# Decode attention on one core: a 0.5 MB weight block loads behind the last values, the TensorE program gets shorter and its opening is ordered by hand

## The chip, the cores and the metric

One NeuronCore of a Trainium2 chip runs the whole kernel. Its engines work side by side and each runs its own instructions in order: TensorE (PE: matrix products, with the weight loads shown as PEld), VectorE (DVE), ScalarE (ACT), GpSimd (POOL) and SyncE (SP), which here only issues transfers. Transfers run on sixteen DMA engines. Data comes from HBM into SBUF, matrix products land in PSUM. The metric is the device time of one execution in microseconds (us): the median of several runs. The profile is one further execution, with the time of every instruction.

## The reference

One token (`x`, 512 values) passes an attention layer over a window of 4096 cached positions for 32 heads of 128, and a small gating network.

```python
xn = layernorm(x)
q = (xn @ wq).reshape(32, 128)                  # wq: 512 x 4096
k, v = k_cache[:, -4096:, :], v_cache[:, -4096:, :]   # 32 heads x 4096 x 128, bf16
p = softmax(q . k * 128**-0.5)                  # per head, over 4096 positions
s = concat(p @ v) @ wo                          # wo: 4096 x 512
h = gelu(layernorm(xn) @ w1); hs = shift(h) @ w2
x1 = xn + hs                                    # with one token the shifted h is all zeros
g = silu(x1 + gelu(layernorm(x1) @ w3) @ w4)    # w3: 512 x 1376
out = x + s * g
```

The window is 32 MB of keys and 32 MB of values, each read once.

## The kernel before

The 32 heads are worked in eight groups of four (`G = 4`). A group's keys are one tile `kv` of 128 partitions by 128 columns of 128 values (4 MB); its values are another. A stage `s` of the main loop takes the keys of group `s` and the values of group `s - 2` (`LAG = 2`).

**Scores.** The first `nd(g)` columns of a group go to DVE in four parts: `k_vector` multiplies by the query (L321) and adds up (L323). The other columns go to PE and ACT in batches of at most eight: `k_turn` transposes on PE (L339) and copies on ACT (L342), `k_scores` multiplies (L350). `nd` is 64 for group 0 and for group 7, 80 for the rest. `sm_own` (ACT, L359), `sm_max` (DVE, L364 and L366), `sm_turn` (PE L372, DVE L374 and L376) and `sm_exp` (PE L381, ACT L384 and L388) make the exponentials `pT`. `sm_den` (PE, L394) adds their sums over partitions and `sm_rden` (DVE, L399) inverts them, once a group.

**Values.** `v_wide` (PE, L427) multiplies `pT` with the values into the one accumulator `ov`, ACT copies it (L433), `v_turn` transposes it (PE, L444), `v_add` adds (DVE, L450) and `v_out` scales by the inverted sum (L471 on DVE for the later groups). The last group is different: its values come in three pieces by the column bounds `cuts`; the last piece goes through `v_part` (PE, L461), straight into the output tile `oT`.

**Output weights.** `wo` is used in four blocks of heads: 0-15, 16-23, 24-27 and 28-31. For the first three, `ox_spread` (DVE, L482) and `ox_pick` (PE L490, DVE L492 and L496) rearrange the heads' outputs to fit the layout in which `wo` was loaded, and `y_wide` (PE, L518) multiplies into the row accumulator `yr`; ACT copies that into `y_sum` (L640), and `rows_add` (PE, L155) adds it to `y_ps`. The last four heads are multiplied singly by `y_head` (PE, L155). Then DVE multiplies by the gate (L651), adds `x` (L653), and the result is stored.

**Order.** All large loads but `wq` go through one helper on SP's queue (L76), in program order: `w2`, `w3`, `w4`, then keys and values as the stages ask for them, each held back until its buffer is free. Key tiles have three buffers, of which one is given to `wo` of heads 0-23 from stage 5 on; value tiles have two, in the space of the opening's weights (`wts`). `wq` goes through ACT's queue. In the main loop the order on PE, DVE and ACT is that of the program (`manual_schedule`). Ahead of the loop (layer norm, query, gate network) Tile's scheduler orders the instructions. Most short PSUM results share one buffer, `misc`: an instruction that writes into it waits until the one before has been read.

**Warm-up.** `warm(3)` (L507) issues three products with zeros, 128 x 512, once ahead of the values of group 6 and once ahead of those of group 7.

Of the kernel before, what the change touches and what calls it, by code (L numbers as in the profile page):

```python
# [8 lines left out]
P = 128  # L9
# [9 lines left out]
G = 4  # L19
# [7 lines left out]
def kernel(  # L27
# [153 lines left out]

    x_f = small.tile([P, KC], FP32, name="x_f")
# [16 lines left out]

    q_row = wts.tile([P, H // G, 2, Dh], BF16, name="q_row")  # L200
    q_bc = small.tile([P, H // G, Dh], BF16, name="q_bc")
    qr = [ps_tr.tile([P, 4, Dh], FP32, tag="pt", name="qr_ps") for _ in range(2)]
    for b in range(2):
        zeros(qr[b][:])
        for c in range(KC):
            wc = wq_sb[:, c, :].rearrange("p (g a d) -> p g a d", a=G, d=Dh)
            for a in range(G):
                nc.tensor.matmul(qr[b][32 * a:32 * a + 1], lhsT=xq_bf[:, c:c + 1], rhs=wc[:, 4 * b:4 * b + 4, a, :],  # L208
                                 start=False, stop=(c == KC - 1), skip_group_check=True)
    nc.scalar.copy(out=q_row[:, 0:4, 0, :], in_=qr[0][:])  # L210
    nc.vector.tensor_copy(out=q_row[:, 4:8, 0, :], in_=qr[1][:])  # L211
    for b in range(2):
        qb_ps = ps_tr.tile([P, 4, Dh], FP32, tag="pt", name="qb_ps")
        nc.tensor.matmul(qb_ps[:], lhsT=sel[:].rearrange("k b a -> k (b a)"), rhs=q_row[:, 4 * b:4 * b + 4, 0, :],
                         start=True, stop=True)
        nc.scalar.copy(out=q_bc[:, 4 * b:4 * b + 4, :], in_=qb_ps[:])
# [11 lines left out]
    shifted_bf = small.tile([P, KC], BF16, name="shifted_bf")  # L228
    nc.vector.memset(shifted_bf[:], 0.0)
    hs_ps = ps_misc.tile([P, KC], FP32, tag="misc", name="hs_ps")  # L230
    for j in range(KC):
        for c in range(KC):
            nc.tensor.matmul(hs_ps[:, j:j + 1], lhsT=w2_sb[:, c, j::4],
                             rhs=shifted_bf[:, c:c + 1], start=(c == 0), stop=(c == KC - 1))
    x1_f = small.tile([P, KC], FP32, name="x1_f")
    nc.vector.tensor_tensor(out=x1_f[:], in0=xn_f[:], in1=hs_ps[:], op=ALU.add)
    xc3, _, rstd3 = ln_stats(x1_f[:], "z3")
    z3_bf = small.tile([P, KC], BF16, name="z3_bf")
    nc.vector.tensor_scalar(out=z3_bf[:], in0=xc3[:], scalar1=rstd3[:], scalar2=None, op0=ALU.mult)

    xn_row = small.tile([P, P], FP32, name="xn_row")
    nc.vector.tensor_scalar(out=xn_row[:], in0=x_row[:], scalar1=negmean[:], scalar2=rstd[:],
                            op0=ALU.add, op1=ALU.mult)

    a_ps = ps_misc.tile([P, 3, P], FP32, tag="misc", name="a_ps")
    zeros(a_ps[:])
    for c in range(KC):
        wc = w3_sb[:, c, 0:10 * P].rearrange("p (q r) -> p r q", r=10)
        parts = [(j, a_ps[32 * j:32 * j + 1, :, :], wc[:, 3 * j:3 * j + 3, :]) for j in range(3)]
        parts += [(3, a_ps[96:97, 0, :], wc[:, 9, :]), (3, a_ps[96:97, 1, 0:96], w3_sb[:, c, 10 * P:F])]  # L250
        for j, dst, w in parts:
            nc.tensor.matmul(dst, lhsT=z3_bf[:, c:c + 1], rhs=w, start=False, stop=(c == KC - 1),
                             skip_group_check=True)
    a_row = wts.tile([P, 3, P], BF16, name="a_row")
    nc.scalar.activation(out=a_row[:], in_=a_ps[:], func=ACT.Gelu_apprx_tanh)  # L255
    at_ps = ps_misc.tile([P, 3, P], BF16, tag="misc", name="at_ps")
    for m in range(3):
        nc.tensor.transpose(at_ps[:, m, :], a_row[:, m, :], ident_bf[:])
    a_bf = small.tile([P, 3, 4], BF16, name="a_bf")
    nc.vector.tensor_copy(out=a_bf[:], in_=at_ps[:, :, 0:P:32])  # L260

    hr_ps = ps_misc.tile([P, KC, P], FP32, tag="misc", name="hr_ps")
    zeros(hr_ps[:])
    terms = [(shifted_bf[:, c:c + 1], w2_sb[:, c, :]) for c in range(KC)]
    for i in range(11):
        n = P if i < 10 else 96
        terms.append((a_bf[0:n, i % 3, i // 3:i // 3 + 1], w4_sb[0:n, i, :]))
    for i, (col, w) in enumerate(terms):
        r = 32 * (i % 4)
        nc.tensor.matmul(hr_ps[r:r + 1].rearrange("r j n -> r (j n)"), lhsT=col, rhs=w, start=False,  # L270
                         stop=(i >= len(terms) - 4), skip_group_check=True)
# [10 lines left out]

    make_masks(16)
    make_masks(8)
    make_masks(4)

    y_ps = ps_y.tile([P, P], FP32, name="y_ps")
    rows_open(y_ps)  # L290

# [16 lines left out]
    def nd(g):  # L308
        return 64 if g == 0 or g >= LATE else 80
# [68 lines left out]
    def sm_exp(g):  # L378
# [7 lines left out]
        s["sum"] = sm_pool.tile([P, G], FP32, tag="sum", name="sum")  # L386
# [4 lines left out]
    def sm_den(g):  # L391
        s = st[g]
        s["den"] = ps_misc.tile([P, G], FP32, tag="misc", name="den_ps")
        nc.tensor.matmul(s["den"][:], lhsT=ones_f[:], rhs=s["sum"][:], start=True, stop=True)  # L394

    def sm_rden(g):
        s = st[g]
        s["rden"] = sm_pool.tile([P, G], FP32, tag="rden", name="rden")
        nc.vector.reciprocal(out=s["rden"][:], in_=s["den"][:])  # L399
# [64 lines left out]
    def v_out(g):  # L464
# [5 lines left out]
        if g >= NG - 5:  # L470
            nc.vector.tensor_tensor(out=o_blk[b][:, c:c + G], in0=st[g]["oT"][:], in1=st[g]["rden"][:],  # L471
                                    op=ALU.mult)
            return
# [30 lines left out]
    def warm(n):  # L504
        wm = ps_s.tile([P, 4, P], FP32, tag="sT", name="wm")
        for _ in range(n):
            nc.tensor.matmul(wm[:], lhsT=zero_bf[:], rhs=zero_bf[:].unsqueeze(1).to_broadcast([P, 4, P]),  # L507
                             start=True, stop=True)

# [12 lines left out]
    def y_head(h):  # L522
# [3 lines left out]
    cuts = (0, 64, 96, CP)  # L526
    region = tc.manual_schedule(engines={mybir.EngineType.PE, mybir.EngineType.DVE,
                                         mybir.EngineType.Activation})
    region.__enter__()
    v_pool = None  # L530
    for s in range(NG + LAG):
# [8 lines left out]
        if last:  # L540
            v = load_kv(v_pool, A_v_cache, h, cuts)
            for r in (H - G, H - 2):
                load_rows(r, 2)
        elif h >= 0:
            v = load_kv(v_pool, A_v_cache, h)
# [4 lines left out]
        if h == 5:  # L550
            load_wo(1)
            load_wo(2)

        if s < NG:
# [11 lines left out]
            if s == 7:  # L566
                v_turn(h - 1)
                v_add(h - 1)
                v_out(h - 1)
            elif s > 1:  # L570
                sm_den(s - 2)
                sm_rden(s - 2)
# [4 lines left out]
            if s == 7:  # L577
                sm_den(h)
                sm_rden(h)
# [38 lines left out]
        elif s == NG:  # L618
# [3 lines left out]
            y_wide(1, False)  # L622
            sm_den(NG - 2)
            sm_rden(NG - 2)
            y_wide(0, False)
            warm(3)
            v_wide(h, v)
            sm_den(NG - 1)
            sm_rden(NG - 1)
# [4 lines left out]
        else:  # L634
            v_open(h)
            warm(3)
            v_wide(h, v, cuts[1], last=False)
            ox_pick(2)
            y_wide(2, True)
            nc.scalar.copy(out=y_sum[:], in_=yr[0][:].rearrange("p j n -> p (j n)"))  # L640
            v_wide(h, v, cuts[2], cuts[1])
            v_turn(h)
            v_add(h)
            rows_add(y_ps, ind, y_sum, False)
            v_part(h, v, cuts[2], CP)
            v_out(h)
            for r in range(H - G, H):
                y_head(r)
    region.__exit__(None, None, None)
    y = small.tile([P, P], FP32, name="y")  # L650
# [34 lines left out]
```

## Time and profile before

| what | value |
|---|---|
| median of 3 runs | 193.45 us (193.33 to 193.55) |
| profiled execution, span from first to last instruction | 191.2 us |
| busy: PE, DVE, ACT | 116.4, 150.9, 89.2 us |
| moved by DMA | 79.02 MB, mean 413 GB/s over the span |
| mean granted TensorE clock | 0.72 |
| last piece of the last values in use on PE | from 186.38 us |
| `y_head` products | 187.59 to 188.01 us |
| store of the result issued | 188.68 us |

The profiled execution has a span of 191.2 us; the median lies 2.25 us above it, time outside the first and last instruction. Times in the views count from the span's start. A row of a timeline gives start, duration, engine, source line and operation, the tiles written and read, and in brackets how long the engine sat idle before it and what ended the wait. "PEclk" is the share of the full TensorE clock that was granted.

### The profile page before, as it was taken

To read this page: it belongs to the slowest core of one execution; us is meant where nothing else is said; L and a number is where in the kernel's file an instruction comes from. 1 tells how busy PE (TensorE), PEld (TensorE's weight loads), DVE (VectorE), ACT (ScalarE), POOL (GpSimd) and SP (SyncE) were. 2 spreads that over 40 slices of the span, in tenths; PEclk is the share of its full clock that TensorE was granted. 3 is DMA by queue.
4 is the path that set the end of the run, shared out by engine and by line. 5 is a ranking of instruction groups with operands and counts; after the bars stand their busy time and mean duration, and the time that the engine had idled before them with its cause. 6 is when DMAs were issued, how large, how long until landed. Compare 5 with 4: busy or idle time off the path is not lost.

```text
span 191.2 us, 2839 instructions
## 1 busy us (share of the span) xinstructions
PE 116.4 (61%) x1159; PEld 74.2 (39%) x1159; DVE 150.9 (79%) x175; ACT 89.2 (47%) x191; POOL 2.3 (1%) x11
## 2 busy tenths in 40 slices
PE   1653754989825368256845772680888189739762
PEld 0430222767614334143334441540763077313322
DVE  1660159979999999999999999999999999980111
ACT  2001370888794076427464564542475148733120
POOL 2110000000000000000000000000000000000000
PEclk9999695555755557955695588557567858975998
DMA  6999999999999999999999999999999998999990
GB/s 211 447 430 404 431 418 439 439 439 437 432 434 439 432 429 432 432 439 432 422 432 432 418 422 418 452 439 435 439 432 434 435 432 372 471 425 405 420 371 32
DMA packets 4572, 79.02 MB, mean 413 GB/s; under 512 B 624, under 2 KB 1232, under 8 KB 1488
## 3 DMA queue, kind: packets, MB, share of 16 engines
q1 hardware_dynamic: 4264, 74.65, 91.6%
q10 hardware_dynamic: 296, 4.20, 5.1%
q8 instruction: 9, 0.15, 0.3%
q14 instruction: 3, 0.02, 0.0%
HBM read 78.84 MB, written 0.00 MB: 412 GB/s over the span
## 4 chain that ended last, share of the span: by engine, by line
DVE 46%; DMA 43%; PE 5%; ACT 3%; issue 1%; SPq 1%; ACTq 0%; DVEq 0%
DMA kv<-in_A_k_cache_dram 31%; DVE S L323 28%; DVE prod L321 15%; DMA kv<-in_A_v_cache_dram 10%; ACT kt L342 3%; DMA x_bf<-in_A_x_dram 2%; PE pt L339 2%; PE ov L427 1%; DVE m L366 1%; DVE S L364 1%; SPq L76 1%; PE sT L350 1%; DVE mx L374 1%; PE oT L461 1%; PE ot_ps L444 0%
## 5 line engine op out<-in xcount | busy, mean ns | idle before, releaser
L323 DVE TENSOR_REDUCE S<-prod 128x20 f32<-128x2560 bf16 (+1 forms) x32 | 86.0, 2686 | 1.1
L342 ACT COPY kt<-pt 128x1024 bf16<-128x1024 bf16 x52 | 51.2, 1013 | 40.4 <-PE pt L339 38.7
L339 PE MATMUL pt<-ident_f,kv 128*128 128x128 f32 x208 | 46.7, 376 | 10.8 <-DMA kv<-in_A_k_cache_dram 10.8
L321 DVE TENSOR_TENSOR prod<-kv,q_bc 128x2560 bf16<-128x2560 bf16 (+1 forms) x32 | 45.4, 1418 | 3.9 <-DMA kv<-in_A_k_cache_dram 3.7
L339 PEld LDWEIGHTS pt<-ident_f,kv 128*128 128x128 f32 x208 | 34.2, 196 | 14.4 <-DMA kv<-in_A_k_cache_dram 10.5
L350 PE MATMUL sT<-q_pair,kt 128*128 128x8 bf16 x416 | 19.4, 170 | 15.7 <-ACT kt L342 15.5
L350 PEld LDWEIGHTS <-kt 128*128 128x128 bf16 x416 | 16.4, 104 | 26.8 <-ACT kt L342 25.8
L427 PE MATMUL ov<-kv,pT 128*16 128x512 bf16 x248 | 22.0, 515 | 1.4 <-DMA kv<-in_A_v_cache_dram 1.4
L388 ACT ACTIVATE pT<-S,mb 128x128 bf16<-128x128 f32 x32 | 13.9, 573 | 0.3
L372 PE MATMUL mt_ps<-ident_f,m 128*1 128x128 f32 x8 | 2.9, 359 | 17.4 <-DVE rden L399 16.9
L433 ACT COPY ov_sb<-ov 128x512 f32<-128x512 f32 x8 | 4.7, 586 | 17.1 <-PE ov L427 17.1
L427 PEld LDWEIGHTS <-pT 128*16 128x16 bf16 x248 | 6.9, 109 | 13.2 <-issue 11.4
L359 ACT ACTIVATE own<-sT,par 128x48 f32<-128x48 f32 (+1 forms) x32 | 7.5, 356 | 3.7 <-PE sT L350 3.7
L444 PE MATMUL ot_ps<-ident_f,ov_sb 128*128 128x128 f32 x32 | 7.1, 359 | 2.9 <-ACT mb L384 1.9
L211 DVE CAST q_row<-qr_ps 128x512 bf16<-128x512 f32 x1 | 0.7, 692 | 9.9 <-PE qr_ps L208 9.9
L388 ACT ACTIVATION_READ_ACCUMULATOR pT<-S,mb 128x1 f32 x32 | 8.3, 258 | 0.0
L372 PEld LDWEIGHTS mt_ps<-ident_f,m 128*1 128x1 f32 x8 | 0.6, 80 | 17.9 <-DVE rden L399 17.2
L399 DVE RECIPROCAL rden<-den_ps 128x4 f32<-128x4 f32 x8 | 1.4, 175 | 7.0 <-PE den_ps L394 7.0
L381 PE MATMUL mb_ps<-md,par_t 5*128 5x4 f32 x16 | 3.9, 311 | 4.1 <-DVE md L376 4.1
L255 ACT ACTIVATE a_row<-a_ps 128x384 bf16<-128x384 f32 x1 | 0.5, 491 | 12.0 <-remote 12.0
L444 PEld LDWEIGHTS ot_ps<-ident_f,ov_sb 128*128 128x128 f32 x32 | 4.5, 178 | 3.9 <-ACT mb L384 2.3
L208 PE MATMUL qr_ps<-wq_sb,xq_bf 128*1 128x512 bf16 x32 | 3.1, 566 | 3.7 <-DMA wq_sb<-in_A_wq_dram 3.7
(122 smaller groups left out, 81.6 us busy)
## 6 DMA issues: line engine op xcount, KB each, us to landing
kv<-in_A_k_cache_dram SPq DMA_DIRECT2D x7, 4096.0 KB, 31.3
kv<-in_A_v_cache_dram SPq DMA_DIRECT2D x7, 4096.0 KB, 30.6
wq_sb<-in_A_wq_dram ACTq DMA_DIRECT2D x1, 4096.0 KB, 17.6
kv<-in_A_k_cache_dram SPq DMA_DIRECT2D x2, 2048.0 KB, 27.4
wo<-in_A_wo_dram SPq DMA_DIRECT2D x1, 2048.0 KB
kv<-in_A_v_cache_dram SPq DMA_DIRECT2D x1, 2048.0 KB
kv<-in_A_v_cache_dram SPq DMA_DIRECT2D x2, 1024.0 KB, 17.6
w_sb<-in_B_w_dram SPq DMA_DIRECT2D x1, 1376.0 KB, 9.1
```

Source lines behind the costliest of these rows:

```text
L321: nc.vector.tensor_tensor(out=prod[:, 0:m, :], in0=kn[:, rows, :], in1=q_bc[:, g:g + 1, :].to_broadcast([P, m, Dh]), op=ALU.mult)
L323: nc.vector.tensor_reduce(out=st[g]["S"][:, rows], in_=prod[:, 0:m, :], axis=AX.X, op=ALU.add)
L339: nc.tensor.transpose(pt[:, i, :], kn[:, c:c + 2, :].rearrange("p c d -> p (c d)").bitcast(FP32), ident_f[:])
L342: nc.scalar.copy(out=kts[b][:, 0:n, :], in_=pt[:, 0:n, :].bitcast(BF16))
L350: nc.tensor.matmul(st[g]["sT"][:, c:c + 2, :].rearrange("p c a -> p (c a)"), lhsT=kt[:, i, l::2], rhs=q_pair[:, g, l, :], start=(l == 0), ...
L359: nc.scalar.mul(s["own"][:, 0:m, a], s["sT"][:, 0:m, a], par[:, a:a + 1])
L372: nc.tensor.transpose(mt_ps[:], s["m1"][:], ident_f[:])
L381: nc.tensor.matmul(mb_ps[:], lhsT=par_t[:].rearrange("k b a -> k (b a)"), rhs=md[:], start=True, stop=True)
L388: nc.scalar.activation(out=s["pT"][:, :, a], in_=s["S"][:], func=ACT.Exp, scale=scale, bias=mb[:, a:a + 1], accum_out=s["sum"][:, a:a + 1])
L427: nc.tensor.matmul(ov[r:r + 4 * G], lhsT=s["pT"][:, c:c + 4, :].rearrange("p i a -> p (i a)"), rhs=v[:, c:c + 4, :], start=(i < 4), stop=( ...
L433: nc.scalar.copy(out=s["ov_sb"][:], in_=ov[:])
L444: nc.tensor.transpose(ot_ps[:, step * j:step * j + P], s["ov_sb"][:, j, :], ident_f[:])
```

## The change

It has these parts.

1. **Load and products of `wo` of heads 24-27.** The 0.5 MB load is no longer issued in the stage of the values of group 5, but behind the three pieces of the last values and ahead of the two loads of `wo` for heads 28-31. Its products go singly into `y_ps`, between the last `v_out` and the `y_head` products, and no longer through `y_wide`. The `y_wide` of heads 16-23 moves from stage 8 to stage 9 and is the last into `yr`.
2. **Pieces of the last values**: bounds 64 and 104 in place of 64 and 96.
3. **No `warm`.**
4. **Group 0 gives 80 columns to DVE**, not 64.
5. **Denominators by pairs of groups**: `sm_den` runs for groups 1, 3, 5 and 7, makes the inverse for two groups, and `sm_rden` is gone. For groups 4 and 5 it stands in stage 7 between `v_add` and `v_out` of group 4.
6. **Opening.** PE and ACT follow program order from the layer norm on. The `w2` products are four rows of 512 with a copy and four transposes, and stay in the accumulator that the `w4` products then add to (before: sixteen products of width 1, and again four rows later). The `w3` products are sixteen, not twenty, with a different split of the 1376 columns; their transposes are two 32-bit ones. The program has the query's products behind the `w3` products.

```diff
+    order = tc.manual_schedule(engines={mybir.EngineType.PE, mybir.EngineType.Activation})
+    order.__enter__()
     x_f = small.tile([P, KC], FP32, name="x_f")
...
+    hr_ps = ps_s.tile([P, KC, P], FP32, tag="sT", name="hr_ps")
+    zeros(hr_ps[:])
...
+    for c in range(KC):
+        hr_add(0, shifted_bf[:, c:c + 1], w2_sb[:, c, :], False)
+    hs_row = wts.tile([1, D], FP32, name="hs_row")
+    nc.scalar.copy(out=hs_row[:], in_=hr_ps[0:1].rearrange("p j n -> p (j n)"))
+    hs_ps = ps_misc.tile([P, KC], FP32, tag="misc", name="hs_ps")
+    for j in range(KC):
+        nc.tensor.transpose(hs_ps[:, j:j + 1], hs_row[0:1, j::4], ident_f[0:1, 0:1])
...
     for b in range(2):
+        if b == 1:
+            a_turn()
         qb_ps = ps_tr.tile([P, 4, Dh], FP32, tag="pt", name="qb_ps")
...
     def nd(g):
-        return 64 if g == 0 or g >= LATE else 80
+        return 64 if g >= LATE else 80
...
     def sm_den(g):
-        s = st[g]
-        s["den"] = ps_misc.tile([P, G], FP32, tag="misc", name="den_ps")
-        nc.tensor.matmul(s["den"][:], lhsT=ones_f[:], rhs=s["sum"][:], start=True, stop=True)
-
-    def sm_rden(g):
-        s = st[g]
-        s["rden"] = sm_pool.tile([P, G], FP32, tag="rden", name="rden")
-        nc.vector.reciprocal(out=s["rden"][:], in_=s["den"][:])
+        den = ps_misc.tile([P, 2 * G], FP32, tag="misc", name="den_ps")
+        nc.tensor.matmul(den[:], lhsT=ones_f[:], rhs=st[g - 1]["sums"][:], start=True, stop=True)
+        rden = sm_pool.tile([P, 2 * G], FP32, tag="rden", bufs=2, name="rden")
+        nc.vector.reciprocal(out=rden[:], in_=den[:])
+        for i in range(2):
+            st[g - 1 + i]["rden"] = rden[:, G * i:G * i + G]
...
-    cuts = (0, 64, 96, CP)
-    region = tc.manual_schedule(engines={mybir.EngineType.PE, mybir.EngineType.DVE,
-                                         mybir.EngineType.Activation})
+    cuts = (0, 64, 104, CP)
+    region = tc.manual_schedule(engines={mybir.EngineType.DVE})
...
             v = load_kv(v_pool, A_v_cache, h, cuts)
+            load_wo(2)
             for r in (H - G, H - 2):
                 load_rows(r, 2)
...
             load_wo(1)
-            load_wo(2)
...
             if s == 7:
                 v_turn(h - 1)
                 v_add(h - 1)
+                sm_den(h)
                 v_out(h - 1)
-            elif s > 1:
+            elif s in (3, 5):
                 sm_den(s - 2)
-                sm_rden(s - 2)
...
             if s == 7:
-                sm_den(h)
-                sm_rden(h)
                 keys(4, nb - 2)
...
             sm_exp(NG - 1)
-            y_wide(1, False)
-            sm_den(NG - 2)
-            sm_rden(NG - 2)
             y_wide(0, False)
-            warm(3)
             v_wide(h, v)
             sm_den(NG - 1)
-            sm_rden(NG - 1)
...
             v_open(h)
-            warm(3)
+            y_wide(1, True)
+            nc.scalar.copy(out=y_sum[:], in_=yr[0][:].rearrange("p j n -> p (j n)"))
             v_wide(h, v, cuts[1], last=False)
             ox_pick(2)
-            y_wide(2, True)
-            nc.scalar.copy(out=y_sum[:], in_=yr[0][:].rearrange("p j n -> p (j n)"))
             v_wide(h, v, cuts[2], cuts[1])
+            rows_add(y_ps, ind, y_sum, False)
             v_turn(h)
             v_add(h)
-            rows_add(y_ps, ind, y_sum, False)
             v_part(h, v, cuts[2], CP)
             v_out(h)
+            for t in range(blocks[2][1]):
+                rows_add(y_ps, ox_blk[2][:, t:t + 1], wo_blk[2][:, t, :], False)
             for r in range(H - G, H):
                 y_head(r)
```

## The prediction

> **What bounds the kernel now.** I read the page's slices first, then the chain in order of time, then half-microsecond windows at the end, then the issues in the timeline.
>
> ```profile
> DMA  6999999999999999999999999999999998999990
> GB/s 211 447 430 404 431 418 439 439 439 437 432 434 439 432 429 432 432 439 432 422 432 432 418 422 418 452 439 435 439 432 434 435 432 372 471 425 405 420 371 32
> ```
>
> The DMA engines are busy in all slices but the first and last, near 430 GB/s; 79.02 MB at that rate take 184 us of the 191.2. DVE is over 90% busy too, so I ask which of them sets the end:
>
> ```profile
> 167.79 18.54 DMA kv<-in_A_v_cache_dram
> ...
> 186.38 0.97 PE oT L461 x32
> ...
> 187.37 0.17 DVE o L471
> ...
> 187.59 0.42 PE y_ps L155 x16
> ...
> 188.04 0.30 DVE y L651
> ```
>
> The last values land at 186.33; 32 products, the scaling and the products of heads 28-31 follow. But two loads stand behind these values, `wo` of heads 28-31. In the windows (time, length, busy PE, PEld, DVE, ACT, POOL, granted clock, DMA share, GB/s) bytes still move:
>
> ```profile
> 187.00:187.50 0.50, 0.33 (x14) 0.24 (x10) 0.13 (x1) 0.00 (x0) 0.00 (x0) 1.00 0.22 68
> 187.50:188.00 0.50, 0.39 (x16) 0.21 (x16) 0.04 (x1) 0.00 (x0) 0.00 (x0) 1.00 0.00 0
> ```
>
> The trace's landing marks put these two loads at 186.95 and 187.61. So two paths end together: the values' chain (scaled at 187.54) and the last bytes (187.61). Only an edit that shortens both gains.
>
> ```profile
> 130.88 1.30 SPq L76 DMA_DIRECT2D kv<-in_A_v_cache_dram  x1
> 132.22 1.06 SPq L76 DMA_DIRECT2D wo<-in_A_wo_dram  x2
> 166.55 1.83 SPq L76 DMA_DIRECT2D kv<-in_A_v_cache_dram  x3
> 168.43 1.10 SPq L76 DMA_DIRECT2D wo_rows<-in_A_wo_dram  x2
> ```
>
> Is the queue ever empty? The last values are issued at 166.55, held until PE has used those of group 5; the values of group 6 land at 176.5 (PE starts on them at 176.56), so about 10 us of work were still queued. Adding 4.19 MB for each issue and dividing by 430 GB/s gives 10 us or more of backlog at every other issue. The transfers are one unbroken stream, and DVE has no say in its end as long as issues slip by less than that.
>
> **The change, part by part.**
>
> *Load of 0.5 MB moved back.* On SP's queue it passes the values of group 6 and of group 7. 0.52 MB at 430 GB/s is 1.2 us, so both come 1.2 us earlier, and `wo` of heads 28-31 stays where it was: the sum of bytes ahead of it is the same. PE begins on the three pieces at 181.50, 183.93 and 186.37 before (2 MB, 1 MB, 1 MB; 2.4 us a MB). With the new bounds (2, 1.25, 0.75 MB): 180.3, 183.3, 185.1. Then the 0.5 MB at 186.35, the rows of heads 28-29 at 186.95, of 30-31 at 187.61.
>
> *The tail.* `v_part` has 24 products, not 32: 0.97 x 24/32 = 0.73, so 185.1 to 185.85, scaled by 186.1. That chain ended at 187.54, so it gains 1.4 us. The sixteen products for heads 24-27 wait for 186.35 and take about 0.4 us (16 of the same shape, 187.59: 0.42), ending 186.8, ahead of the next landing. The products of heads 28-29 follow 186.95; those of 30-31 wait for 187.61: 0.05 us hand-off (as 186.33 to 186.38), then eight: one alone takes 0.218 us (L155 row), the other seven (0.42 - 0.22)/15 = 0.013 each, 0.31 in all. End 187.97 against 188.01. Gain: 0.04 us. The values' chain gains 1.4, but the bytes do not.
>
> *Group 0 on DVE.* By shape, a part of 20 columns costs 1.484 + 2.820 = 4.30 us, one of 16 costs 1.219 + 2.285 = 3.50. Four parts: 3.2 us more.
>
> ```profile
> 38.63 2.29 DVE L323 TENSOR_REDUCE S<-prod 128x16 f32<-128x2048 bf16 x1
> 41.91 1.49 DVE L321 TENSOR_TENSOR prod<-kv,q_bc 128x2560 bf16<-128x2560 bf16 x1 [0.99 <-DMA kv<-in_A_k_cache_dram]
> 134.17 1.49 DVE L321 TENSOR_TENSOR prod<-kv,q_bc 128x2560 bf16<-128x2560 bf16 x1 [0.55 <-DMA kv<-in_A_k_cache_dram]
> ```
>
> DVE waited 0.99 us for the keys of group 1: 2.2 us remain, and every later key load is issued that much later, inside the 10 us. Three reciprocals fewer by stage 6 give back 0.5 (0.175 each), the wait at 134.17 another 0.55: DVE starts group 7 about 1.1 us late. PE and ACT lose two batches of 1.0 us (L342 row) in group 0, in a place where nothing waits for them.
>
> *Denominators.* Four fewer reciprocals (0.7 us of DVE), and one new wait. In stage 7 the denominators now stand on PE right behind `v_turn` and must wait until DVE's `v_add` has read `misc`; DVE then waits for them:
>
> ```profile
> 157.53 0.21 DVE L450 TENSOR_REDUCE oT<-ot_ps 128x4 f32<-128x64 f32 x1
> 159.28 0.36 PE L394 MATMUL den_ps<-sum,ones_f 128*128 128x4 f32 x2
> 161.31 0.17 DVE L399 RECIPROCAL rden<-den_ps 128x4 f32<-128x4 f32 x1
> ```
>
> DVE idles some 0.6 us (0.36 to 0.59 for the two products, and two hand-offs); late by 1.7. Behind the waiting product on PE stand the key batches, which began at 156.9 and now at 159.2; ACT copies at 1.0 us a batch, so `v_wide` of group 5 ends near 168.6 (166.5 before), and the last values are issued at 168.6. The queue runs out at 175.3: hidden, 6.7 us to spare. DVE's last maximum comes at 172.5 (170.6), the last exponentials near 176.3 (174.4), needed from 180.3.
>
> *No `warm`.* Six products, 1.07 and 0.81 us of PE. Their use would be the clock (columns as above):
>
> ```profile
> 172.68:176.09 3.41, 3.41 (x28) 1.14 (x21) 0.18 (x1) 1.64 (x8) 0.00 (x0) 0.50 0.92 394
> 176.09:179.50 3.41, 3.04 (x40) 1.43 (x39) 0.18 (x1) 0.59 (x1) 0.00 (x0) 1.00 0.99 418
> 179.50:182.92 3.42, 2.14 (x24) 0.85 (x22) 0.76 (x5) 0.00 (x0) 0.00 (x0) 1.00 0.97 412
> 182.92:186.33 3.41, 1.98 (x24) 0.73 (x24) 0.39 (x2) 1.17 (x2) 0.00 (x0) 1.00 0.90 359
> ```
>
> The Trainium skill, "TensorE: Matmul & The Clock Gate", Part 1, speaks against this edit: the array runs at half clock until it has been busy through a window of about 3.4 us, and falls back after an idle one. The rows agree (3.41 us busy, then the full grant) and add that windows with 2.14 and 1.98 us busy keep it. By the rule without `warm`: `y_wide` of heads 0-15 from 174.2 takes 1.9, then `v_wide` of group 6 takes 3.7 at half clock (3.4 to 3.5 at 0.53 to 0.55 of it, against 1.90): to 179.8. That itself is a busy window, so the full clock comes by 179.5. I take this case. Then: copy 0.6 and `v_turn` 0.7 to 181.3, eight `y_wide` 0.5, 16 `v_wide` 1.04 to 182.9, the pick 0.2, ten `v_wide` 0.65 from the landing at 183.3 to 184.0, copy 0.65, `v_turn` 0.66 to 185.35, `v_part` 0.73 to 186.1, scaled at 186.35. That still only meets the 0.5 MB landing. By the row (full clock kept) there are 0.5 to 1.8 us more of slack. Both give the same end.
>
> *Opening.* The row form of `w2` costs four products of 0.38, a copy of 0.6 and four small transposes (no such row: between 0.1 us each, as the weight loads of L221, and 0.36, as the transposes of L372; I take 0.15, since they follow each other) in place of 0.67 us: `x1` about 3 us later, near 11.4. The 4.5 us from there to `z3` (8.47 to 13.2 before) end at 16, the `w3` products (2.9 before; sixteen by the same columns 2.5 to 2.9) near 18.9. `wq` lands at 19.9, and DVE starts at 26.09 only because the first keys land then. Hidden; if it came out 1 us longer, the query would move by that, and 1 us of the cover at 26.09 would take it (`q_bc` is done at 25.0).
>
> *Shorter program.* The page lists 9 instruction loads of 16 KB, 0.3% of 16 engines' span, or 1.0 us each on one engine. The Trainium skill, "Runtime: NRT & Kernel Launch", Instruction fetch mechanics, gives 256 instructions a block: 99 fewer are 0.4 of one. The end of a transfer is that of its slowest engine; the marks of the last load spread from 185.64 to 187.61, ten of sixteen after 186.7. Taking the load off one of ten moves the end by 0 to 0.1 us; off the only slowest, up to 1.0. By the row I take 0, by the rule at most 0.4.
>
> **Sum**: -0.04 us on 191.2, nothing outside the span. Median 193.45 - 0.05 = 193.4.
>
> **The cases.** The first is the forecast, the others are its rivals.
> 1. *No change beyond 0.2%* (0.39 us, about what a measurement of this kernel can tell from none): the bytes set the end before and after. For it: the unbroken DMA row, the landing at 187.61. 193.4, own range 193.1 to 193.8. Chance 0.55.
> 2. *The transfers end earlier.* Fewer instruction loads on the slow engines, or the landing of the last rows is no limit and the chain's 1.4 us count. For it: the marks' spread of 2 us; against: ten engines are late. 0.4 to 1.0 us: 192.8. Chance 0.2.
> 3. *Slower: the full clock comes too late on PE.* If it returns only at 186.3, the chain above runs at half clock from 176.1: `v_turn` of group 6 to 181.6, `y_wide` 182.6, `v_wide` 184.5 and 186.0, copy 186.7, `v_turn` 187.4, `v_part` 188.15, scaled 188.4, 32 products 0.6: 189.0, or 1.0 us more: 194.4. It decides once the scaled output comes after 187.1. For it: DVE's 1.9 us and the missing products; against: 3.7 us of `v_wide` fill a window. Chance 0.25.
>
> That the change doesn't move the load is excluded: SP's queue keeps program order.
>
> **Range.** From the middle of rival 2, 192.8, to the price of rival 3, 194.4; some 2 in 10 lie outside.
>
> **What would show it.** Right: last bytes within 0.2 us of 187.6; `v_part` from about 185.1 to 186; the last L155 products waiting for a load; DVE's group 1 starting 2 us later; `v_wide` of group 6 at half clock. Wrong: a DMA slice below 9 in mid-run (an issue came too late), `v_part` ending after 186.8, the granted clock at 0.5 after 182.9, or landings that end at another time than 187.6.

## The result and the profile after

The changed kernel takes 193.82 us (median of 15 runs, 193.52 to 195.31), the kernel before in the same session 193.47 (15 runs, 193.28 to 193.95). The ratio is 1.0037 (95% interval 1.002 to 1.0054): slower by 0.37%. The forecast was no change, 193.4.

Its runs fall into two groups: eight from 193.52 to 193.82 (spans 191.7 to 192.0 us) and seven from 194.63 to 195.31 (spans 192.8 to 193.5). No run of the kernel before is that high (194.36 at most in all sessions). So three numbers have to be explained: the lower group's span is about 0.7 us above the 191.2 of before, the upper one's about 1.2 us above that, and the time outside the span fell: 1.75 us in the profiled execution (194.65 us, span 192.9, so one of the upper group), 1.74 to 1.96 in all kernels made from the changed one but for a few stray runs, against 2.09 to 2.28 in the kernel before. The ratios leave out runs over 1.5% above the fastest of their kernel, which further down are one run of `best_late` and two of `best_k256`; medians and counts include them.

The slices of the page after:

```profile
span 192.9 us, 2736 instructions
...
DMA  6999999999999999999999999999999999999890
GB/s 200 453 434 404 424 425 432 421 435 437 432 428 437 435 435 435 432 435 428 435 432 428 435 428 391 469 428 435 428 418 437 435 421 406 440 425 411 331 372 21
```

The DMA engines are as busy as before, but the slice from about 178.4 to 183.3 moves 331 GB/s. Bytes set the end, as they did before. Two rows of the chain of waits, and the end of the timeline on PE (start, duration, engine, line):

```profile
168.31 3.39 PE ov L436 x31
174.78 14.46 DMA wo_rows<-in_A_wo_dram
```

```profile
177.75 3.63 PE L436 MATMUL ov<-kv,pT 128*16 128x512 bf16 x32
...
187.22 0.74 PE L470 MATMUL oT<-pT,kv 128*128 128x4 bf16 x24 [0.32 <-DVE oT L459]
...
187.93 0.39 PE L155 MATMUL y_ps<-wo,ox 128*1 128x128 bf16 x16
...
188.59 0.38 PE L155 MATMUL y_ps<-wo_rows,o 128*1 128x128 bf16 x8 [0.27 <-DMA wo_rows<-in_A_wo_dram]
...
189.28 0.38 PE L155 MATMUL y_ps<-wo_rows,o 128*1 128x128 bf16 x8 [0.31 <-DMA wo_rows<-in_A_wo_dram]
```

The last rows land at 174.78 + 14.46 = 189.24; before, 187.61. That is 1.63 us of the 1.7 by which the span grew. By the first landing marks of the loads in the trace, 4 MB of values took 9.71 to 9.77 us (before 9.65 to 9.66) and keys 9.67 to 9.70 (before 9.70 to 9.72). By the last marks, the values of group 6 came about 0.65 us late (175.95, where 176.52 less the 1.2 us of the moved load was due), and the loads behind them lost another 1.0. The 1.25 MB piece took 3.97 us (first marks) where `before_cuts104` below needs 3.04.

Stage 7 on DVE and PE before:

```profile
154.07 1.22 DVE L321 TENSOR_TENSOR prod<-kv,q_bc 128x2048 bf16<-128x2048 bf16 x1
...
161.85 0.28 DVE L374 TENSOR_REDUCE mx<-mt_ps 1x4 f32<-1x128 f32 x1 [0.36 <-PE mt_ps L372]
...
164.60 1.90 PE L427 MATMUL ov<-kv,pT 128*16 128x512 bf16 x32
```

The same after, and SP's queue behind it:

```profile
155.95 1.22 DVE L330 TENSOR_TENSOR prod<-kv,q_bc 128x2048 bf16<-128x2048 bf16 x1
...
159.40 0.21 DVE L459 TENSOR_REDUCE oT<-ot_ps 128x4 f32<-128x64 f32 x1
...
159.67 0.60 PE L404 MATMUL den_ps<-sum,ones_f 128*128 128x8 f32 x2 [2.27 <-DVE oT L459]
160.31 0.21 DVE L406 RECIPROCAL rden<-den_ps 128x8 f32<-128x8 f32 x1 [0.69 <-PE den_ps L404]
...
165.33 0.28 DVE L383 TENSOR_REDUCE mx<-mt_ps 1x4 f32<-1x128 f32 x1 [1.17 <-PE mt_ps L381]
...
168.24 3.46 PE L436 MATMUL ov<-kv,pT 128*16 128x512 bf16 x32
```

```profile
171.75 1.83 SPq L76 DMA_DIRECT2D kv<-in_A_v_cache_dram  x3
173.63 0.59 SPq L76 DMA_DIRECT2D wo<-in_A_wo_dram  x1
174.27 0.98 SPq L76 DMA_DIRECT2D wo_rows<-in_A_wo_dram  x2
```

DVE starts group 7 1.9 us late; the denominators wait as forecast and DVE idles 0.69 us, then 1.17 us more ahead of the maximum (0.36 before), which comes 3.5 us late; the values of group 5 start 3.6 us late and take 3.46 us at half clock (1.90 at full clock before); so the last values are issued at 171.75, 5.2 us later than before and 3.1 later than forecast. The clock among these may belong to the execution and not to the change: over the 20 profiles of this document the same product took 1.90 us in nine and 3.2 to 3.6 in eleven, and both kinds occur among kernels made from the one before and from the changed one.

### The profile page after: what moved, and what is told of

It reads as the page before. It is cut to its first block, busy times and chain, and to the rows that moved or that the text cites. A ratio compares the mean times of both kernels' runs of the same rounds, so it can differ in the third digit from the quotient of the medians.

```text
span 192.9 us, 2736 instructions
## 1 busy us (share of the span) xinstructions
PE 117.6 (61%) x1110; PEld 71.8 (37%) x1110; DVE 154.7 (80%) x171; ACT 89.5 (46%) x191; POOL 2.3 (1%) x11
## 4 chain that ended last, share of the span: by engine, by line
DVE 67%; DMA 17%; PE 9%; ACT 3%; issue 1%; SPq 1%; POOL 1%; ACTq 0%; DVEq 0%; POOLq 0%
DVE S L332 41%; DVE prod L330 21%; DMA wq_sb<-in_A_wq_dram 9%; DMA wo_rows<-in_A_wo_dram 7%; PE pt L348 2%; PE qr_ps L261 2%; PE ov L436 2%; ACT kt L351 2%; SPq L76 1%; DVE m L375 1%; DVE S L373 1%; PE qt_ps L276 1%; PE hr_ps L208 1%; ACT q_row L273 1%; DVE mx L383 1%
## 5 line engine op out<-in xcount | busy, mean ns | idle before, releaser
L332 DVE TENSOR_REDUCE S<-prod 128x20 f32<-128x2560 bf16 (+1 forms) x32 | 88.1, 2753 | 1.1
L351 ACT COPY kt<-pt 128x1024 bf16<-128x1024 bf16 x50 | 49.0, 1013 | 32.6 <-PE pt L348 31.2
L330 DVE TENSOR_TENSOR prod<-kv,q_bc 128x2560 bf16<-128x2560 bf16 (+1 forms) x32 | 46.4, 1450 | 1.7 <-DMA kv<-in_A_k_cache_dram 1.4
L348 PE MATMUL pt<-ident_f,kv 128*128 128x128 f32 x200 | 43.1, 364 | 7.6 <-DMA kv<-in_A_k_cache_dram 7.6
L348 PEld LDWEIGHTS pt<-ident_f,kv 128*128 128x128 f32 x200 | 31.4, 188 | 11.0 <-DMA kv<-in_A_k_cache_dram 6.4
L359 PE MATMUL sT<-q_pair,kt 128*128 128x8 bf16 x400 | 18.5, 170 | 14.8 <-ACT kt L351 14.4
L436 PE MATMUL ov<-kv,pT 128*16 128x512 bf16 x250 | 26.3, 591 | 0.3 <-DMA kv<-in_A_v_cache_dram 0.3
L359 PEld LDWEIGHTS <-kt 128*128 128x128 bf16 x400 | 15.5, 103 | 25.6 <-ACT kt L351 24.8
L390 PEld LDWEIGHTS mb_ps<-md,par_t 5*128 5x128 f32 x16 | 3.8, 291 | 16.8 <-issue 13.3
L393 ACT COPY mb<-mb_ps 128x4 f32<-128x4 f32 x8 | 1.3, 163 | 14.7 <-PE mb_ps L390 14.7
```

Of the source, the lines that this page charges most:

```text
L330: nc.vector.tensor_tensor(out=prod[:, 0:m, :], in0=kn[:, rows, :], in1=q_bc[:, g:g + 1, :].to_broadcast([P, m, Dh]), op=ALU.mult)
L332: nc.vector.tensor_reduce(out=st[g]["S"][:, rows], in_=prod[:, 0:m, :], axis=AX.X, op=ALU.add)
L348: nc.tensor.transpose(pt[:, i, :], kn[:, c:c + 2, :].rearrange("p c d -> p (c d)").bitcast(FP32), ident_f[:])
L351: nc.scalar.copy(out=kts[b][:, 0:n, :], in_=pt[:, 0:n, :].bitcast(BF16))
L359: nc.tensor.matmul(st[g]["sT"][:, c:c + 2, :].rearrange("p c a -> p (c a)"), lhsT=kt[:, i, l::2], rhs=q_pair[:, g, l, :], start=(l == 0), ...
L390: nc.tensor.matmul(mb_ps[:], lhsT=par_t[:].rearrange("k b a -> k (b a)"), rhs=md[:], start=True, stop=True)
```

## The experiments

Five theories, with the numbers that the expectations use. Four are for the slower span: **row size** (theory 1: the new 1.25 MB piece moves in 10,240-byte rows, and these are slow); **late issue** (theory 2: a queue that is fed at 171.75 loses time although it is not yet empty); **moved load** (theory 3: moving the 0.5 MB load costs by itself); **address** (theory 4: the value tiles start elsewhere). The built programs show that they do: 159936 and 192704 bytes into each partition, before 160000 and 192768, both multiples of 256. The tiles of the paired sums and inverses take 64 bytes less, and all that lies behind them moves down, `wq` and the `wo` blocks of heads 24 to 31 too. The last, for the time outside the span, is the **length of the program** (theory 5).

"Upper runs" below are those with a span over 0.9 us above the lowest span of the same kernel, so they are not counted from one level in all kernels. Issue times are those of the one profiled execution of each kernel; those of its other runs are not known.

### Row size

```diff
 # after_cuts96: the changed kernel
-    cuts = (0, 64, 104, CP)
+    cuts = (0, 64, 96, CP)
 # before_cuts104: the kernel before
-    cuts = (0, 64, 96, CP)
+    cuts = (0, 64, 104, CP)
```

> The changed kernel with the pieces of the last values cut at 64 and 96 again, as before. Theory 1 (the second piece, now 1.25 MB in rows of 10,240 bytes, moves slowly: its first engine took 3.97 us where 1.25 MB at 430 GB/s are 3.05): the piece of 1 MB takes 2.4 us, the last bytes land 0.8 to 0.9 us earlier than in the changed kernel, time near that of the kernel before plus 0.3 us. Theory 2 (the last values are issued too late, 171.75 against 166.55 us): no change of the issue, time as the changed kernel, +0.3 to +1.8 us from run to run. Theory 3 (the load of 0.5 MB behind the values costs by itself): as theory 2.

> The kernel before with the cut at 104 in place of 96 and nothing else. Theory 1: the 1.25 MB piece moves slowly here too, +0.6 to +0.9 us. Theories 2 and 3: the issue stays at 166.6 us, the piece takes 3.05 us, time as before within 0.2 us (the last part, 24 products in place of 32, could give 0.1).

`after_cuts96`: 194.0 us, ratio 1.0036 (1.0025 to 1.0047); its profile has a normal second piece (2.47 us for 1 MB), but its spans still run from 191.9 to 193.0 (2 upper runs of 18). `before_cuts104`: 193.68, 1.0016 (1.0003 to 1.0029), with 1 upper run of 13, and its 1.25 MB piece takes 3.04 us. Neither bound carries the loss: theory 1 falls as its cause, though a part in how often upper runs come is not excluded (7 of 15 with the new bounds). The 0.2 us of the second kernel lie on PE: in its profile the values' chain ended the span.

### Earlier issue, without and with the old address

```diff
 # after_den_late: stage 7 of the changed kernel
                 v_add(h - 1)
-                sm_den(h)
-                v_out(h - 1)
...
             keys(2, 4)
             if s == 7:
+                sm_den(h)
+                v_out(h - 1)
 # after_nd64: the changed kernel
-        return 64 if g >= LATE else 80
+        return 64 if g == 0 or g >= LATE else 80
 # after_v256: the changed kernel, 64 unused bytes ahead of the value tiles
+    sm_pool.tile([P, 32], BF16, tag="pad2", bufs=1, name="pad2")
 # after_v256_den_nd64: all three
```

> The changed kernel with the denominators of groups 4 and 5 behind the second pair of key batches again (and the scaling of group 4 behind them). Theory 2: PE no longer stands idle 2.3 us in stage 7 and DVE 0.7, the last values are issued at 167 to 169.5 us instead of 171.75, the slow runs (194.6 to 195.3) disappear, time 193.4 to 193.7. Theories 1 and 3: the issue comes earlier but the time stays as in the changed kernel, with its two groups of runs.

> The changed kernel with 64 columns of group 0 on DVE, as before. Theory 2: DVE starts group 7 about 1.9 us earlier (154.1 in place of 155.95), the last values are issued 1 to 2 us earlier than 171.75, most slow runs disappear, time 193.4 to 193.9. Theories 1 and 3: DVE earlier, time as the changed kernel.

> The changed kernel with 64 bytes of unused space ahead of the value tiles, so that they start where they do in the kernel before (address 160000 in a partition, a multiple of 256; the change moved them to 159936). Nothing else differs. Theory 4 (the values and opening weights land slower because their rows in SBUF no longer start on 256 bytes; the trace has 9.71 to 9.77 us for 4 MB of values against 9.66 before): values take 9.66 us again, the last keys land 0.3 to 0.5 us earlier than in the changed kernel (154.0), the lower group of its runs (193.5 to 193.8) moves to 193.1 to 193.4; the upper group stays, since the last values are still issued late. Theory 2 (late issue alone): no change of either group.

> The changed kernel with three parts undone: value tiles on 256 bytes, denominators of groups 4 and 5 behind the second pair of key batches, 64 columns of group 0 on DVE. Theories 2 and 4 together: the last values are issued by 169.5 us, no run above 194, median 193.0 to 193.3, at or below the kernel before. If only theory 2 holds: 193.7 to 193.8, without slow runs. If only theory 4 holds: 193.2 to 193.4 with slow runs.

| kernel | last values issued (profile) | median, us | ratio (95%) | upper runs |
|---|---|---|---|---|
| changed | 171.75 | 193.82 | 1.0037 (1.002-1.0054) | 7 of 15 |
| after_den_late | 170.1 | 193.79 | 1.002 (1.0011-1.003) | 0 of 21 |
| after_nd64 | 171.0 | 193.82 | 1.002 (1.0013-1.0026) | 0 of 22 |
| after_v256 | 171.4 | 194.12 | 1.0033 (1.0015-1.0051) | 16 of 22 |
| after_v256_den_nd64 | 167.9 | **192.84** | **0.997 (0.9959-0.9981)** | 0 of 7 |

Undoing a part of the lateness alone takes the upper runs away and leaves the lower group where it was (spans from 191.7); in `after_nd64` an issue only 0.7 us earlier is enough. Mending the address alone brings four runs down to 192.74 to 193.00 (spans 190.9 to 191.2), lower than expected, but the other eighteen lie between 193.59 and 195.41, and the median is no lower. Both together: every run at 192.66 to 192.98, **faster than the kernel before**. Both losses are real, and each hides most of what mending the other would gain.

Windows of 1 us (time, length, busy PE, PEld, DVE, ACT, POOL, granted clock, DMA share, GB/s) show what a late issue does, in the changed kernel:

```profile
180.00:181.00 1.00, 1.00 (x16) 0.17 (x8) 0.00 (x0) 0.00 (x0) 0.00 (x0) 0.50 0.90 338
181.00:182.00 1.00, 0.86 (x6) 0.47 (x2) 0.10 (x1) 0.57 (x1) 0.00 (x0) 0.66 0.77 266
182.00:183.00 1.00, 0.74 (x9) 0.59 (x13) 0.19 (x2) 0.01 (x1) 0.00 (x0) 1.00 0.79 293
```

and in `after_v256_den_nd64`:

```profile
180.00:181.00 1.00, 1.00 (x24) 0.40 (x16) 0.55 (x3) 0.46 (x1) 0.00 (x0) 1.00 0.97 410
181.00:182.00 1.00, 0.47 (x9) 0.18 (x2) 0.35 (x2) 0.13 (x1) 0.00 (x0) 1.00 1.02 432
182.00:183.00 1.00, 0.00 (x0) 0.00 (x0) 0.00 (x0) 0.00 (x0) 0.00 (x0) 1.00 0.97 404
```

With work queued, the DMA share falls to 0.77. Of the 128 packets of 10,240 bytes of the second piece, 42 took over 0.43 us, up to 0.85, in place of 0.385.

### The address alone, in the kernel before

```diff
+    sm_pool.tile([P, 96], BF16, tag="pad2", bufs=1, name="pad2")   # 192 unused bytes
```

> The kernel before with 192 bytes of unused space ahead of the value tiles: they start at 160192, 192 above a multiple of 256, as in the changed kernel. Theory 4: +0.3 to +0.5 us over the kernel before, the last keys land at 153.8 to 154.0 in place of 153.5. Theory 2: same time as before.

194.22 us (5 runs, 193.91 to 194.32), ratio 1.0039 (1.0027 to 1.0051), twice what was expected. Nothing else in the program differs. The median span is 192.0 against 191.2, and the last bytes land at 188.65 against 187.61. Of that, 0.7 us is there when the values of group 6 land (177.22 against 176.52). The remaining 0.3 fall in the last loads, which this profile issued at 168.5 in place of 166.55 (the product of group 5 took 3.40 us), so lateness may have a part in these. In the trace the median packet of 32,768, 16,384 and 8,192 bytes takes 1.215, 0.614 and 0.312 us in place of 1.213, 0.612 and 0.309. The opening's weights move with the value tiles, since they share the space, and some of their packets are slower too. **The address costs about 0.8 us, with the later issue that came with it.**

The keys start at 128 beyond such a multiple in all these kernels. Does mending that help too?

```diff
 # best_k256: after_v256_den_nd64, keys and values at multiples of 256
+    lead = ctx.enter_context(tc.tile_pool(name="lead", bufs=1))
+    lead.tile([P, 64], BF16, name="lead")
...
-    sm_pool.tile([P, 32], BF16, tag="pad2", bufs=1, name="pad2")
+    sm_pool.tile([P, 96], BF16, tag="pad2", bufs=1, name="pad2")
```

> The kernel with three parts undone, plus unused space of 128 bytes ahead of the key tiles and 128 ahead of the value tiles: the keys too now start on a multiple of 256 bytes (16640 in place of 16512). Theory 4: 4 MB of keys take 9.66 us like the values, not 9.71, nine times 0.05: 0.3 to 0.5 us less, 192.4 to 192.5. Against it (only the values' address mattered): 192.84.

192.69 (22 runs, 192.48 to 195.5), ratio 0.997 (0.9955 to 0.9984), where 192.4 to 192.5 was expected: the lowest runs of all, the last bytes at 187.28 against 187.45, but six upper runs of 22, with an issue at 168.9 in the profile. 0.15 us in the median is inside the spread, so a gain from the keys' address is not shown.

### The issue time, moved by zero products

```diff
 # after_v256_den_nd64, stage 7; N = 4, 8, 12: best_late4, best_late, best_late12
+                wm = ps_s.tile([P, 4, P], FP32, tag="sT", name="wm")
+                for _ in range(N):
+                    nc.tensor.matmul(wm[:], lhsT=zero_bf[:], rhs=zero_bf[:].unsqueeze(1).to_broadcast([P, 4, P]),
+                                     start=True, stop=True)
                 v_wide(h, v)
 # best_late_cuts96: N = 8, and cuts = (0, 64, 96, CP)
```

> The kernel with three parts undone (192.84 us), plus eight products with zeros, 128 x 512, on PE ahead of the values of group 5 in stage 7. They hold those back by 1.7 us at full clock and 3.4 at half, so the last values are issued near 170 to 171.3 us in place of 167.9; nothing else is changed. Theory 2 (a late issue of the last values costs, even while the transfers of group 6 still run): time goes up to 193.3 to 194.5, with the pieces of the last values taking more than 4.85 and 3.05 us on the first engine. Against it (the issue matters only once the queue is empty, at 173.4): 192.8 to 193.0, apart from what a later start of the values' chain on PE costs at the end, which the profile shows.

> The kernel after_v256_den_nd64 with four zero products ahead of the values of group 5 in stage 7, in place of the eight of best_late: the last values are issued about 1.7 us later than in after_v256_den_nd64, near 169.7, and nothing of the computation is left out. Theory 2 (a late issue of the last values slows their transfer, from about 171 on): no run in an upper group, no 10,240-byte packet slower than 0.43 us, median 192.85 to 193.0. The rival (the slowdown comes from the phase in which the queues happen to stand, not from how late the issue is, as best_k256 with an issue at 168.9 and 6 upper runs of 22 would have it): about one run in four 1 us or more above the rest, as with eight products.

> The same with twelve zero products: the last values are issued near 172.8. Theory 2: most runs in the upper group, median 194.0 to 195. The rival (phase of the queues): as with eight products, median 193.1 to 193.4 and about one run in four above 194. If the transfers were hidden until the queue runs out at 175.3, as the prediction had it: 192.9.

> best_late (eight zero products) with the old bounds of the last values (0, 64, 96, 128), so packets of 8,192 bytes in both later pieces. If the slowdown belongs to late issue whatever the packet size: an upper group of about one run in four as in best_late (14 runs, 4 above 194), median 193.2 to 193.5. If it belongs to the packets of 10,240 bytes: no run above 193.9, and the median some 0.2 above that of after_v256_den_nd64 (longer last piece), 193.0.

| zero products | issue (profile) | median, us | ratio (95%) | upper runs |
|---|---|---|---|---|
| 0 | 167.9 | 192.84 | 0.997 (0.9959-0.9981) | 0 of 7 |
| 4 | 167.5 | 192.94 | 0.9976 (0.9965-0.9988) | 2 of 22 |
| 8 | 171.2 | 193.19 | 0.9998 (0.9982-1.0013) | 4 of 14 |
| 8, old bounds | 169.7 | 193.16 | 0.9994 (0.9979-1.0009) | 2 of 14 |
| 12 | 170.4 | 193.80 | 1.0016 (1.0006-1.0026) | 9 of 22 |

Eight are the clearest case. In that profile the product of group 5 takes 1.90 us, the last values are issued at 171.2, 56 of the second piece's 128 packets take over 0.43 us, and the last bytes end the span, 1.3 us later than without the products (187.45):

```profile
174.23 14.53 DMA wo_rows<-in_A_wo_dram
188.76 0.04 issue
188.81 0.41 PE y_ps L156 x7
```

With four I had expected a later issue, and it did not come. In the timeline of `best_late4` the values of group 5 take 1.90 us:

```profile
164.55 1.02 PE L594 MATMUL wm<-zero_bf 128*128 128x512 bf16 x4
165.50 1.90 PE L437 MATMUL ov<-kv,pT 128*16 128x512 bf16 x32
```

Without them, in `after_v256_den_nd64`, the same product starts earlier and ends later:

```profile
164.43 3.42 PE L437 MATMUL ov<-kv,pT 128*16 128x512 bf16 x32
```

That the four products brought the full clock is not shown: the trace of `best_late4` has it granted from 159.1 on, 5.4 us before they start, and `best_blocks` and `best_open_before` took 1.90 us without any.

Beyond four the time grows with the products, though the issue times of the profiles don't: twelve cost 1.0 us of median, a little less than expected. Hidden until 175.3, as the forecast had it, would have been 192.9. Not all of it is transfers: in the profile of twelve the last bytes land at 188.51 (187.45 without), but the chain ends on PE, whose values' chain came later still, at a granted clock of 0.5 from 184.3 on:

```profile
187.50 0.78 PE oT L471 x24
188.28 0.98 PE y_ps L156 x32
```

In six profiles the packets of 10,240 bytes are slow (14 to 69 of the second piece's 128 over 0.43 us); in five of them the last values were issued at 170.4 or later, the sixth is `best_k256`. `after_cuts96`, issued at 171.6 with packets of 8,192 bytes, shows a single one over 0.36 us, and `best_late_cuts96` still has two upper runs. Lateness raises the chance of a slow transfer but does not decide it. Upper runs come without packets of 10,240 bytes too; whether such packets make them more frequent is not settled.

### The moved load alone

```diff
 # after_wo_early: from the changed kernel; best_wo_early: from after_v256_den_nd64
             v = load_kv(v_pool, A_v_cache, h, cuts)
-            load_wo(2)
...
             load_wo(1)
+            load_wo(2)
```

> The changed kernel with the load of the 0.5 MB block at its old place in stage 7, its products still single and last. Theory 3 (moving the load costs by itself): time back near the kernel before, 193.4 to 193.5. Theory 2: with 1.2 us more of queue ahead of the last values the late issue is covered, so the upper group of runs shrinks or goes; the lower group stays at 193.5 to 193.8. Theory 4: lower group unchanged.

> The kernel with three parts undone, but the load of the 0.5 MB block at its old place, its products still single and last. The last values land 1.2 us later (186.1), 24 products, scaling and 32 products follow: end of the products near 187.9 to 188.1 against 187.8. If the moved load gains as the prediction had it: +0.1 to +0.3 us. If it gains more (+0.95 us in the changed kernel with late issue): +0.6 to +1.0.

`after_wo_early` 194.77 (1.0066, 1.0049 to 1.0082), `best_wo_early` 194.14 (1.0032, 1.002 to 1.0044). Taken out of the change, the move is missed by 0.95 and 1.3 us, more than any expectation had: theory 3, that the moved load costs by itself, falls. But put alone into the kernel before, with no `warm` and the new order of the tail (`before_tail`):

```diff
             v = load_kv(v_pool, A_v_cache, h, cuts)
+            load_wo(2)
...
-            load_wo(2)
...
-            y_wide(1, False)
...
-            warm(3)
...
+            y_wide(1, True)
+            nc.scalar.copy(out=y_sum[:], in_=yr[0][:].rearrange("p j n -> p (j n)"))
...
+            for t in range(blocks[2][1]):
+                rows_add(y_ps, ox_blk[2][:, t:t + 1], wo_blk[2][:, t, :], False)
```

> The kernel before with the parts of the tail alone: the load of 0.5 MB behind the last values, its products among the last, y_wide of heads 16-23 one stage later, no warm; bounds of the last values, denominators, group 0 and opening as before. By the prediction: last landing at 187.6 and 0.04 us less, 193.4. If the tail is what shortens the time outside the span: 1.75 to 1.9 outside and 193.05. By the rival of the late clock: 194.0 or more.

it gives 193.37 against 193.4, ratio 1.0001 (0.9992 to 1.0009). Its timeline ends as forecast, `v_part` at 184.9, and the last rows at 187.51:

```profile
184.88 1.02 PE L461 MATMUL oT<-pT,kv 128*128 128x4 bf16 x32 [0.41 <-DMA kv<-in_A_v_cache_dram]
...
187.55 0.38 PE L155 MATMUL y_ps<-wo_rows,o 128*1 128x128 bf16 x8 [0.36 <-DMA wo_rows<-in_A_wo_dram]
```

The difference between the two tests is in the chain of `best_wo_early`:

```profile
176.52 0.04 issue
176.56 3.59 PE ov L437 x30
...
183.12 1.71 PE ov L437 x13
...
186.37 0.67 PE ot_ps L454 x4
187.03 0.02 issue
187.06 0.24 DVE oT L460
187.30 0.04 issue
187.34 0.74 PE oT L471 x24
188.09 0.68 PE y_ps L156 x32
```

Here the values' chain ends the span, not the bytes (its last rows land at 187.59). From the landing of group 6's values at 176.52 the chain waits for no load. The granted clock is 0.5 until 184.8 (in `after_v256_den_nd64` it is full from 178.3), so PE reaches the second piece at 184.87, although this one, 0.25 MB longer, landed at 184.40 (183.89 before). Copy, transposes and sum follow; `v_part` starts at 187.34 although its piece landed at 186.23, and 32 products come behind it (0.68 us) where the kernel before has 16 (0.42). With the load moved, `v_part` starts at 185.55. The move pays for what other parts of the same change, and in this execution the late clock, add to PE's tail. No run puts `warm` back alone, so the share of the clock is not known.

### Outside the span

```diff
 # best_blocks: after_v256_den_nd64 and 20 tiny zero products at the start
+    for _ in range(20):
+        nc.tensor.matmul(fill[:], lhsT=zero_bf[:], rhs=zero_bf[:, 0:KC], start=True, stop=True)
 # best_open_before: after_v256_den_nd64 with the whole opening of the kernel before
 # before_pairs: the kernel before with the new sm_den and the paired sums (v_out of group 4 behind them), values at 160000
```

> The kernel with three parts undone, plus 20 products of width 4 with zeros on PE at the very start, where PE idles until 4.9 us: 40 instructions more on PE. The kernels of the changed family have 1.8 us outside the span, those of before 2.16. Theory 5 (this goes by the length of the TensorE program: 2286 instructions here and 2325 in the longest that has 2.12): outside the span 2.1 to 2.2 us, time 193.2, span unchanged at 191.0. Against it (another part of the opening): 1.8 us outside, 192.84.

> The kernel after_v256_den_nd64 with the opening of the kernel before (w2 in column form, w3 in five parts, the order of PE and ACT there chosen by the planner); the starts of the value tiles stay at multiples of 256. If the 0.35 us less outside the span belong to the new opening: time minus span 2.1 to 2.2, median 193.2. If not: 1.8 outside the span, median 192.8. Either way the opening is hidden, as the prediction had it: the span stays at 190.9 to 191.2 and DVE's first product starts within 0.1 us of where it does in after_v256_den_nd64.

> The kernel before with the denominators made for pairs of groups, nothing else (for groups 4 and 5 at the place where those of group 5 stood; 64 unused bytes keep the value tiles at 160000). Five kernels with one or another part of the change undone all kept the shorter time outside the span (1.75 to 1.9 us, before 2.1 to 2.3). If the pairs are what shortens it: 1.75 to 1.9 outside, median 193.1. If not: 2.1 to 2.3 and 193.4, since the span is set by the bytes. By the step of the prediction on the denominators alone: no change of the span.

`best_blocks`: 193.0 (0.9976, 0.9969 to 0.9984), 2828 instructions in its trace, 1.74 to 1.91 us outside. `before_cuts104` has 2827 and a median of 2.16: theory 5 falls. `best_open_before`: 192.96 (0.9972, 0.996 to 0.9983), 1.76 to 1.92: not the opening, and the opening is hidden (spans 191.0 to 191.2, against 190.8 to 191.2 with the new one). `before_tail` kept 2.10 to 2.29. `before_pairs`: **193.01 (0.998, 0.9972 to 0.9989), 1.74 to 1.87 outside**, span 191.2 as before. The paired denominators take 0.35 us off, all of it outside the first and last instruction. Why, no view shows.

## Why the prediction was wrong, step by step

- **Unbroken stream, bytes set the end.** Right: the last rows ended the span before and after. But "the sum of bytes ahead of it is the same", so the same landing, left out the pace. The pairs shrank the small tiles, the value tiles lost their address, and that costs about 0.8 us (`before_v192`). This step failed first; it makes the lower group, whose span is 0.7 us longer.
- **"Hidden, 6.7 us to spare".** This failed second and makes the upper group, about 1.2 us of span. DVE was 1.9 us late and not 1.1; the maximum of group 6 came 3.5 late, where DVE was to be 1.7 behind; the product of group 5 was taken at its old 1.90 us and took 3.46 (half clock, as in `after_v256_den_nd64`, where no denominators wait), so the issue came at 171.75 and not 168.6. Above all the cover was taken as whole until the queue is empty at 175.3; `best_late`, issued at 171.2, lands its last bytes 1.3 us late.
- **Tail: 0.04 us.** `before_tail` agrees for the part alone, within its interval of 0.09% either way. In the changed kernel the move is worth about 1 us: the new bounds, the sixteen products more at the end and, in the profile of `best_wo_early`, the half clock lengthen the values' chain. The step took the chain of before as the one without the move.
- **"Nothing outside the span".** Wrong by 0.35 us in favour, from the pairs. Lower group: 0.7 longer span less 0.35 leaves the 0.3 us or so that those runs are slower; with the upper runs among them the median is 0.35 above. That the result lies so near the forecast is luck: two unforeseen losses and an unforeseen gain.
- **No `warm`; the rival of the late clock.** The product of group 6 took 3.63 us at half clock (forecast 3.7), and the full clock came at 181.7 (forecast by 179.5, from a start 1.7 us earlier). PE was late, `v_part` ended at 187.96, but the bytes came later, so the rival that gave the right sign, at 194.4, had another mechanism. Its own mechanism does show in `best_wo_early`, where the clock comes at 184.8 and PE ends the span. And the windows that the prediction saw keep the clock with 2.14 and 1.98 us of busy PE make no rule: in the profile before, the one from 165.9 to 169.3 has 1.79 us busy, and the clock falls at its end.
- **Opening, group 0, shorter program.** The opening is hidden (`best_open_before`). Group 0 is part of the late issue (0.7 us of it in the profile of `after_nd64`). The shorter program as such gives nothing clear of the intervals (`best_blocks`, longer again: 193.0 against 192.84, with no more time outside the span); the 0.4 us that the prediction allowed for it was an estimate, and does not show.
- **Rival of an earlier end of transfers, 192.8.** It did not happen in the changed kernel; with address and issue mended, 192.84 comes from the pairs (about 0.35) and some 0.15 us of earlier landing.

What was not settled: why the packets of a late-issued load slow down while others are queued, and in some executions only; why a start off a multiple of 256 costs time; and what the pairs shorten.

## What to carry to other kernels

Where transfers are the bound, compare the start addresses of the large tiles in both programs before calling the bytes unchanged; a small tile that shrinks can cost more than the edit gains. Slack of a transfer is not the time until its queue runs empty: vary the issue time, over many runs, and read where the cost begins. A part that is worth nothing alone can be worth 1 us beside the others, so test parts both ways, added to the old kernel and taken out of the new one.

## What the runs showed of the hardware

- Value tiles that start 192 bytes past a multiple of 256 in each partition: 9.71 to 9.77 us for 4 MB in the changed kernel, 9.71 to 9.73 in `before_v192`, in place of 9.65 to 9.66; 0.8 us for the whole kernel in `before_v192`, with nothing else changed.
- A load issued late, but with work still queued: DMA share down to 0.77, 42 of 128 packets of 10,240 bytes over 0.43 us in place of 0.385, in some executions only.
- 32 products of 128 x 512 in stage 7: 1.90 us or 3.2 to 3.6, by the clock granted in that execution (nine and eleven of 20 profiles).
- Pairing the denominators shortens the time outside the span from 2.14 to 1.81 us (medians), at the same span.
